# Retention and two mixture-of-experts layers on one core: domain rows, bank sums, low parts, gate passes and tables

## Chip, cores and metric

One core of a Trainium2 chip runs the whole kernel in one launch. The metric is the device time of that launch in microseconds (us). The engines by their names in the profile: PE (TensorE, matmul), DVE (VectorE), ACT (ScalarE), POOL (GpSimd) and SP (SyncE, which here issues every DMA). PEld is PE's weight load, which runs beside the matmuls. A "q" behind an engine's name marks its sequencer (SPq issues DMAs).

## What is computed

```python
def _attn_ref(q, k, v):                 # q, k, v: (2, 8, 768, 64)
    ...
    for t in range(S):
        state = gamma[None, :, None, None] * state + np.einsum('bhd,bhe->bhde', k[:, :, t], v[:, :, t])
        y[:, :, t] = scale * np.einsum('bhd,bhde->bhe', q[:, :, t], state)

def _moe_ref(x, w_gate, w1, w2):        # x: (1536, 512), 8 experts of 512 x 1024 and 1024 x 512
    logits = x @ w_gate
    logits = logits - logits.max()
    P = np.exp(logits)
    for _ in range(8):
        P /= P.sum(1, keepdims=True) + 1e-09
        P /= P.sum(0, keepdims=True) + 1e-09
        P *= N / E
    for e in range(E):
        out += P[:, e:e + 1] * (np.maximum(x @ w1[e], 0.0) @ w2[e])

def _moe2_ref(x, domain_probs, w1, w2): # 4 experts of the same size
    p = domain_probs / (domain_probs.sum(-1, keepdims=True) + 1e-09)
    for e in range(E):
        out += p[:, e:e + 1] * (np.maximum(x @ w1[e], 0.0) @ w2[e])
```

Retention gives x, the first layer takes it, the second takes the first one's output.

## The kernel before

**Retention.** Twelve chunks of 128 positions, six for each of the two sequences (NCK = 6). Round i of the loop (L369 to L398) scales the running state (`att_decay`, POOL), loads and prepares chunk i+2 (`load_att`, `att_prep`: ACT copies q into a padded tile qab, POOL makes ks and qs), computes the scores of chunk i+1 (`att_scores`: PE L251, DVE mask L252), adds chunk i to the state (`att_state`: PE L271, DVE L279 or L284) and computes its outputs (`att_out`: PE L295 and L298) into one of two PSUM banks called chain. The first chunk of a sequence (0 and 6) has no L295, the last (5 and 11) no state. What turns outputs into the first layer's x runs one or two rounds later: `todo[:4]` reads the bank (`first_half` for the first three chunks of a sequence; b12, a split, `sums13`, `sums24` with L152 for the others), `late` splits the sums TA and TB, which then lie in SBUF, into a high part (ACT, L77) and a low part (L78).

**Number format.** Every operand of the expert matmuls is split into a high part and the rest, so that one product is three matmuls (L494). The products of 2 x 2 blocks are made with seven instead of eight multiplications; the sums for that are `+S..`, `+T..` for the weights (`sum_of`, L117), TA and TB for x. `split_hi` (ACT, L124) and `split_lo` (L128) split the weights. The lows of A11, A22, A12 and S1 of the very first weights run on DVE, S2, S3 and S4 on POOL.

**Order.** The code is written in the order in which each engine runs it: every engine takes its instructions strictly in that order, and SP its DMAs. In the retention the order is the loop's. Behind it each call is an event with a position in slots; one slot is one group of six matmuls (about 1.04 us), a unit has 28 slots. A unit is half an expert's hidden width for one sequence, 48 in all; unit k begins at position 28k. First come seven products M1 to M7, with r = 0 and 1, then N1 to N7; helpers between them on DVE, ACT and POOL have fitted positions (`UNIT_AT`, `W_AT`). Named in what follows: m22 (POOL, L617, multiplies by the factors, whose tile is also the high part of A12), h12 and l12 (high part on ACT, low part on POOL, L554, of A12), a4, l3, l4 (DVE), u2 and c1n (ACT copies), e2 to e7 (`add`, bank into the accumulator), g11 (DVE, writes the temporary a11).

**Around the retention's end.** x of chunks 10 and 11 isn't finished in the loop: eight calls left over run in unit 0 at -1, -0.5, 0, 0.5 and 13.8 to 16.8 (L874). Their TA and TB tiles are the accumulators' buffers, which unit 0's e6, e5, e4 and e2 overwrite.

**Gate.** `gate_steps` is a generator that runs in the slots of units 0 to 3 (`GATE_AT`): logits, exponential by a polynomial, then eight passes of row sum and division (L454 to L457), column sum by a matmul with ones (L462) and division (L464 to L468). A pass takes five of these slots. At its end `keep_rows` transposes the factors and writes them to DRAM with eight DMAs (L317), at position 22.9 of unit 3. Unit 4, the first of expert 1, reads them back as rows broadcast over the partitions (`fac`, L526, at position 24 of unit 3). The w2 weights of unit 4 are loaded at 25.1. All these DMAs are SP's.

**Domain factors.** `load_small` and `prep_small` do the same for the second layer's factors in rounds 1 and 4, with eight row DMAs in round 4.

**Tables.** `small` holds identity (128 columns), ones (128) and the decay tables and selector (20); it comes with one DMA between the first loads.

## Time and profile before

| | |
|---|---|
| median of 3 runs | 1535.44 us (1533.57 to 1536.02) |
| the profiled execution's own time, its span | 1535.97 us, 1534.0 us |
| mean granted clock of PE | 0.992 |
| busy, of the span | PE 98%, PEld 95%, DVE 72%, ACT 49%, POOL 68% |
| chain of work that ended last, by engine | PE 86%, POOL 5%, DVE 4%, issue 2%, DMA 1%, ACT 1%, SPq 1% |
| retention | 0 to 86.7 us |
| units 0 to 3 with the gate | 86.7 to 230 us |

How to read it: a busy PE is one with a matmul under way; the granted clock beside it says at which speed. A stage table gives per stretch of time how long each engine was busy. A timeline row names start, length, engine, line, operation and tiles, and in brackets how long the engine was idle before it and which instruction ended that wait. A wait for several things is put down to the one that came last.

### The profile page before, as it was taken

To read this page: it belongs to the slowest core of one execution; us is meant where nothing else is said; L and a number is where in the kernel's file an instruction comes from. 1 tells how busy PE (TensorE), PEld (TensorE's weight loads), DVE (VectorE), ACT (ScalarE), POOL (GpSimd) and SP (SyncE) were. 2 spreads that over 40 slices of the span, in tenths; PEclk is the share of its full clock that TensorE was granted. 3 is DMA by queue.
4 is the path that set the end of the run, shared out by engine and by line. 5 is a ranking of instruction groups with operands and counts; after the bars stand their busy time and mean duration, and the time that the engine had idled before them with its cause. 6 is when DMAs were issued, how large, how long until landed. Compare 5 with 4: busy or idle time off the path is not lost.

```text
span 1534.0 us, 24223 instructions
## 1 busy us (share of the span) xinstructions
PE 1497.3 (98%) x8682; PEld 1463.1 (95%) x8682; DVE 1106.0 (72%) x2096; ACT 755.7 (49%) x1612; POOL 1037.6 (68%) x903
## 2 busy tenths in 40 slices
PE   9799998999999999999999999998999999999998
PEld 6589898999999999999999999998999999999998
DVE  4765986777677677677677767779767777776776
ACT  3454433554554445455455455456655544554452
POOL 5374756867667668668668568569977676686682
PEclk9899999999999999999999999999999999999999
DMA  7410102212111211211211211211121111112112
GB/s 238 139 34 15 49 9 72 63 39 66 49 38 54 61 38 45 70 38 38 77 38 39 76 39 39 63 52 38 39 72 43 38 57 58 38 47 68 38 39 93
DMA packets 97289, 86.23 MB, mean 56 GB/s; under 512 B 9233, under 2 KB 85137, under 8 KB 97169
## 3 DMA queue, kind: packets, MB, share of 16 engines
q1 hardware_dynamic: 97168, 84.69, 18.2%
q8 instruction: 68, 1.11, 0.3%
q14 instruction: 53, 0.43, 0.1%
HBM read 81.45 MB, written 3.22 MB: 55 GB/s over the span
## 4 chain that ended last, share of the span: by engine, by line
PE 86%; POOL 5%; DVE 4%; issue 2%; DMA 1%; ACT 1%; SPq 1%; DVEq 0%; POOLq 0%; ACTq 0%
PE ps L494 47%; PE chain L494 36%; POOL w L128 1%; POOL raw L117 1%; POOL h L554 1%; DMA q<-in_qT 1%; PE chain L295 1%; PE ps L251 1%; PE chain L298 1%; DVE ps L481 1%; DVE acc L481 1%; PE ps L349 1%; DMA raw<-in_w2a 0%; POOL ev L617 0%; DVE acc L152 0%
## 5 line engine op out<-in xcount | busy, mean ns | idle before, releaser
L494 PE MATMUL ps<-h,w 128*128 128x384 f32 x2304 | 433.7, 335 | 4.7 <-POOL h L554 4.4
L494 PE MATMUL ps<-xh,w 128*128 128x384 f32 x1536 | 429.9, 335 | 1.6 <-ACT ev L478 1.6
L494 PEld LDWEIGHTS ps<-h,w 128*128 128x128 f32 x2304 | 402.1, 188 | 7.9 <-POOL h L554 6.4
L128 POOL TENSOR_TENSOR w<-raw,w 128x512 fp32r<-128x512 f32 x262 | 349.7, 1339 | 61.2 <-ACT w L124 61.1
L494 PE MATMUL chain<-xh,w 128*128 128x384 f32 x1152 | 333.3, 336 | 7.1 <-ACT ev L478 5.5
L494 PE MATMUL chain<-h,w 128*128 128x384 f32 x1728 | 334.5, 336 | 3.9 <-DVE acc L481 2.5
L554 POOL TENSOR_TENSOR h<-ev,h 128x384 fp32r<-128x384 f32 x288 | 292.5, 1030 | 44.3 <-ACT h L478 44.2
L494 PEld LDWEIGHTS chain<-h,w 128*128 128x128 f32 x1728 | 303.0, 189 | 6.2 <-DVE acc L481 3.7
L617 POOL TENSOR_TENSOR ev<-ev,fac 128x384 f32<-128x384 f32 x96 | 98.3, 1024 | 306.3 <-DVE ps L613 305.6
L494 PEld LDWEIGHTS ps<-xh,w 128*128 128x128 f32 x1536 | 282.0, 189 | 2.3 <-ACT ev L478 2.3
L124 ACT ACTIVATE w<-raw 128x512 fp32r<-128x512 f32 x336 | 205.1, 624 | 157.9 <-POOL raw L117 133.1
L117 POOL TENSOR_TENSOR raw<-raw 128x512 f32<-128x512 f32 x188 | 244.5, 1300 | 21.1 <-POOL w L128 13.0
L494 PE MATMUL ps<-xl,w 128*128 128x384 f32 x768 | 257.3, 335 | 0.0
L481 DVE TENSOR_TENSOR acc<-chain,acc 128x384 f32<-128x384 f32 x272 | 150.6, 554 | 106.9 <-PE chain L494 105.6
L494 PEld LDWEIGHTS chain<-xh,w 128*128 128x128 f32 x1152 | 211.9, 188 | 9.8 <-ACT ev L478 6.4
L554 DVE TENSOR_TENSOR h<-ps,h 128x384 fp32r<-128x384 f32 x384 | 211.0, 550 | 13.7 <-ACT h L478 4.6
L478 ACT ACTIVATE h<-ps 128x384 fp32r<-128x384 f32 x384 | 186.1, 487 | 65.3 <-DVE ps L481 61.7
L494 PE MATMUL chain<-xl,w 128*128 128x384 f32 x576 | 193.1, 335 | 1.8 <-POOL xl L758 1.8
L478 ACT ACTIVATE chain<-ps 128x384 f32<-128x384 f32 x192 | 91.9, 479 | 206.6 <-DVE acc L481 182.2
L481 DVE TENSOR_TENSOR acc<-ps,acc 128x384 f32<-128x384 f32 x272 | 145.4, 548 | 46.6 <-PE ps L494 46.6
L478 ACT ACTIVATE h<-ev 128x384 fp32r<-128x384 f32 x288 | 149.7, 520 | 46.4 <-DVE ev L557 40.9
L494 PEld LDWEIGHTS ps<-xl,w 128*128 128x128 f32 x768 | 144.7, 188 | 0.0
(122 smaller groups left out, 1242.0 us busy)
## 6 DMA issues: line engine op xcount, KB each, us to landing
fac<-rows SPq DMA_DIRECT2D x46, 384.0 KB
raw<-in_w1a SPq DMA_DIRECT2D x128, 128.0 KB
raw<-in_w2a SPq DMA_DIRECT2D x64, 256.0 KB
raw<-in_w1b SPq DMA_DIRECT2D x64, 128.0 KB
raw<-in_w2b SPq DMA_DIRECT2D x32, 256.0 KB
q<-in_qT SPq DMA_DIRECT2D x12, 256.0 KB
k<-in_kT SPq DMA_DIRECT2D x12, 256.0 KB
v<-in_vN SPq DMA_DIRECT2D x12, 256.0 KB
```

The costliest lines, as they stand in the source:

```text
L117: eng.tensor_tensor(out=raws[s, k], in0=raws[s, a], in1=raws[s, b], op=op)
L124: nc.scalar.activation(out=t[0], in_=raws[s, k], func=AF.Copy)
L128: eng.tensor_tensor(out=lo, in0=raws[s, k], in1=f32(hi), op=ALU.subtract)
L251: nc.tensor.matmul(p_[:, j * 2 * CK:(j + 1) * 2 * CK], t["k"][:, pr, :], z[:, pr], start=True, stop=True)
L295: nc.tensor.matmul(o, S[c % 2][:, pr, :], t["qs"][:, pr, :], start=True, stop=False, skip_group_check=True)
L298: nc.tensor.matmul(o[64 * z:64 * z + 64], t["v"][:, h * 64:(h + 1) * 64], t["a"][:, h, :], start=(c == 0), stop=True, skip_group_check=True)
L349: nc.tensor.matmul(p_[:, 0:TH], l, r, start=(n == 0), stop=(n == len(mm) - 1))
L478: copy, relu = (lambda o, i, f=f: nc.scalar.activation(out=o, in_=i, func=f) for f in (AF.Copy, AF.Relu))
L481: nc.vector.tensor_tensor(out=out, in0=in0, in1=in1, op=op)
L494: nc.tensor.matmul(p_, l, r, start=(first and n == 0), stop=(n == len(mm) - 1), skip_group_check=True)
L554: eng.tensor_tensor(out=lo, in0=src, in1=f32(hi), op=ALU.subtract)
L617: nc.gpsimd.tensor_tensor(out=a22, in0=a22, in1=self.g_[:, 1], op=ALU.mult)
```

## The change

- `prep_small` in round 4 only transposes the domain factors (`turn_rows`); their eight row DMAs are issued at the end of round 7 (NCK + 1), behind the loads of chunk 9.
- In the retention loop `todo[:4]` runs ahead of `late`.
- The low parts of TA and TB of chunks 10 and 11 run on DVE instead of POOL, at 15.8, 17.0 (chunk 11), 18.5 and 20.3 (chunk 10).
- The low parts of A11, A22, A12 and S1 of the first weights run on POOL instead of DVE.
- The gate tile G gets a ninth column holding EPS and a further row block holding EPS / 128, so that both sums contain EPS; the sixteen additions L455 and L466 go. Per pass there is one slot less: four.
- The small tables come with two DMAs: 20 columns at the old place, identity and ones behind the loads of chunk 1.

```diff
@@ -143,7 +143,7 @@
-    def second_half(key, b, j, pb, xa, xb, b21, eng):
+    def second_half(key, b, j, pb, xa, xb, b21):
@@ -163,7 +163,7 @@
         return [b12, lambda: split(*x["B22"], pb[:, 2:4]), sums13, sums24,
-                lambda: split(*x["TA"], xa, eng), lambda: split(*x["TB"], xb, eng)]
+                lambda: split(*x["TA"], xa), lambda: split(*x["TB"], xb)]
@@ -208,7 +208,7 @@
         small = per.tile([P, C_END - C_ID], F32, name="small")
-        nc.sync.dma_start(out=small, in_=cst[:, C_ID:C_END])
+        nc.sync.dma_start(out=small[:, C_G - C_ID:], in_=cst[:, C_G:C_END])
         ident = small[:, 0:P]
@@ -219,6 +219,7 @@
         load_att(1, ("kn", "v"))
+        nc.sync.dma_start(out=small[:, 0:C_G - C_ID], in_=cst[:, C_ID:C_G])
@@ -302,14 +303,17 @@
             xa = xs.pop(i - TPH)
-            return second_half(1, b, c - TPH, quads(p_), xa, xs.pop(i), xa[:, 2:4], nc.gpsimd if i >= len(chunks) - 2 else nc.vector)
+            return second_half(1, b, c - TPH, quads(p_), xa, xs.pop(i), xa[:, 2:4])
-        def keep_rows(t, key, tmp):
+        def turn_rows(t, tmp):
             nc.vector.transpose(tmp, t.rearrange("p t e -> p e t"))
+            return tmp
+        def keep_rows(key, tmp):
             to = rows[key].rearrange("(c f) (t q i) -> q f t c i", f=2, q=4, i=32)
@@ -335,7 +339,7 @@
             nc.vector.tensor_tensor(out=dp_[:, 0:NT], in0=dpr, in1=s.unsqueeze(2).to_broadcast([P, NT, E2]), op=ALU.mult)
-            keep_rows(dp_, 2, ap1.tile([P, 16 * E2], F32, name="dpt"))
+            return turn_rows(dp_, ap1.tile([P, 16 * E2], F32, name="dpt"))
@@ -375,7 +379,7 @@
             att_state(i)
-            for f in late + todo[:4]:
+            for f in todo[:4] + late:
                 f()
@@ -383,7 +387,9 @@
             if i == 4:
-                prep_small()
+                dpt = prep_small()
+            if i == NCK + 1:
+                keep_rows(2, dpt)
             if i == NCK + 3:
@@ -395,14 +401,17 @@
                     split_hi(0, k)
-                    split_lo(0, k, nc.gpsimd if i > 9 else nc.vector)
+                    split_lo(0, k, nc.gpsimd)
         att.close()
-        G_ = per.tile([P, 16, E1], F32, name="G")
+        G_ = per.tile([P, 16, E1 + 1], F32, name="G")
         nc.gpsimd.memset(G_, 0.0)
-        G = G_[:, 0:NT]
-        Gf = G.rearrange("p t e -> p (t e)")
+        nc.gpsimd.memset(G_[:, 0:NT, E1:], EPS)
+        nc.gpsimd.memset(G_[:, NT:NT + 1, 0:E1], EPS / P)
+        G = G_[:, 0:NT, 0:E1]
@@ -417,10 +426,10 @@
             t = spare(4)
-            r_ = lgs = t[:, 0:NT * E1]
-            n_ = pw = t[:, NT * E1:2 * NT * E1]
-            nc.vector.tensor_copy(lgs, pl)
-            q_ = Gf
+            r_ = lgs = t[:, 0:NT * E1].rearrange("p (t e) -> p t e", e=E1)
+            n_ = pw = t[:, NT * E1:2 * NT * E1].rearrange("p (t e) -> p t e", e=E1)
+            nc.vector.tensor_copy(lgs, pl.rearrange("p (t e) -> p t e", e=E1))
+            q_ = G
             yield
@@ -448,26 +457,23 @@
             stt(out=q_, in0=q_, scalar=1.0, in1=pw, op0=ALU.add, op1=ALU.mult)
-            nc.vector.tensor_tensor(out=Gf, in0=q_, in1=q_, op=ALU.mult)
+            nc.vector.tensor_tensor(out=G, in0=q_, in1=q_, op=ALU.mult)
             yield
             for _ in range(8):
-                nc.vector.tensor_reduce(out=rs, in_=G, axis=AX.X, op=ALU.add)
-                ts(out=rs, in0=rs, scalar1=EPS, scalar2=None, op0=ALU.add)
+                nc.vector.tensor_reduce(out=rs, in_=G_[:, 0:NT], axis=AX.X, op=ALU.add)
                 nc.vector.reciprocal(out=rs, in_=rs)
                 yield
-                yield
-                p_ = pg[:, 0:NT * E1]
-                nc.tensor.matmul(p_, ones, Gf, start=False, stop=True, skip_group_check=True)
+                p_ = pg[:, 0:(NT + 1) * E1]
+                nc.tensor.matmul(p_, ones, G_[:, 0:NT + 1, 0:E1], start=False, stop=True, skip_group_check=True)
                 yield
                 nc.vector.memset(p_, 0.0)
-                ts(out=cs, in0=cs, scalar1=EPS, scalar2=None, op0=ALU.add)
                 nc.vector.reciprocal(out=cs, in_=cs)
                 yield
-            keep_rows(G_, 1, evp.tile([P, 16 * E1], F32, tag="a11", name="gt"))
+            keep_rows(1, turn_rows(G_[:, :, 0:E1], evp.tile([P, 16 * E1], F32, tag="a11", name="gt")))
@@ -871,7 +877,7 @@
                         at(k * L + pos, to_x2, un.b, name, c)
-        for pos, f in zip((-1, -0.5, 0, 0.5, 13.8, 14.8, 15.8, 16.8), todo[:4] + late + todo[4:]):
+        for pos, f in zip((-1, -0.5, 0, 0.5, 15.8, 17.0, 18.5, 20.3), todo + late):
             at(pos, f)
```

## Rows read from the trace of the kernel before

**Rows 1.** Stage table: us; busy PE, PEld, DVE, ACT, POOL (instructions); granted clock; DMA share; GB/s.

```profile
0.00:12.54 12.54, 9.43 (x52) 5.94 (x52) 4.04 (x7) 4.42 (x6) 4.33 (x12) 1.00 0.87 299
12.54:40.25 27.71, 27.70 (x224) 19.36 (x224) 15.77 (x33) 8.94 (x16) 15.88 (x16) 1.00 0.65 195
40.25:46.01 5.76, 0.00 (x0) 0.00 (x0) 0.00 (x0) 1.28 (x3) 0.00 (x0) 0.78 0.56 162
46.01:65.50 19.49, 16.68 (x112) 11.72 (x112) 18.55 (x30) 11.65 (x23) 10.08 (x8) 0.71 0.51 175
111.20:117.74 6.54, 3.86 (x16) 3.84 (x16) 1.83 (x4) 3.05 (x7) 5.98 (x6) 0.80 0.28 81
147.00:229.00 82.00, 76.27 (x430) 72.80 (x429) 70.81 (x162) 38.91 (x85) 51.70 (x45) 1.00 0.09 27
232.80:242.00 9.20, 4.23 (x15) 4.23 (x16) 2.67 (x4) 3.10 (x7) 4.42 (x4) 0.81 0.52 149
319.00:1040.00 721.00, 720.06 (x4150) 719.42 (x4149) 524.34 (x975) 357.22 (x766) 496.22 (x431) 1.00 0.17 51
```

**Rows 2.** Timeline, 30 to 46 us: start, us, engine, line, operation, tiles, [idle before].

```profile
30.09 0.43 SPq L190 DMA_DIRECT2D kn<-in_kN  x1
...
35.69 1.04 POOL L234 TENSOR_TENSOR ks<-kn,small 128x512 f32<-128x512 f32 x1 [4.03 <-DMA kn<-in_kN]
...
38.19 0.30 DVE L312 STREAM_TRANSPOSE dpt<-dp 128x64 f32<-128x64 f32 x1
...
38.52 3.19 SPq L317 DMA_DIRECT2D rows<-dpt  x8
...
41.82 0.36 SPq L190 DMA_DIRECT2D q<-in_qT  x1
...
44.68 0.63 ACT L230 ACTIVATE qab<-q 64x512 f32<-64x512 f32 x1 [10.13 <-DMA q<-in_qT]
...
46.01 3.78 PE L251 MATMUL ps<-qab,k 128*128 128x256 f32 x8 [5.76 <-ACT qab L231]
```

**Rows 3.** Timeline, 46 to 57 us: two pairs of L78, and PE's wait.

```profile
46.64 1.29 DVE L78 TENSOR_TENSOR xl<-acc,xh 128x512 fp32r<-128x512 f32 x2 [6.98 <-ACT xh L77]
...
52.63 2.67 DVE L78 TENSOR_TENSOR xl<-acc,xh 128x512 fp32r<-128x512 f32 x2
...
56.88 0.54 PE L295 MATMUL chain<-qs,S 128*128 128x128 f32 x2 [2.81 <-DVE acc L152]
```

**Rows 4.** Timeline, 105 to 114 us: L78 on POOL, and PE's wait.

```profile
105.66 2.56 POOL L78 TENSOR_TENSOR xl<-acc,xh 128x512 fp32r<-128x512 f32 x2
...
113.90 1.92 PE L494 MATMUL ps<-h,w 128*128 128x384 f32 x8 [2.68 <-POOL h L554]
```

**Rows 5.** Timeline of SP, 225 to 231 us.

```profile
225.72 3.21 SPq L317 DMA_DIRECT2D rows<-gt  x8
229.64 0.88 SPq L526 DMA_DIRECT2D fac<-rows  x2
```

**Rows 6.** Chain that ended last, in order of time: start, us, what.

```profile
5.35 5.75 DMA q<-in_qT
...
230.56 6.13 DMA raw<-in_w2a
```

**Rows 7.** Groups by line and shape, DVE, 0 to 120 us: count | busy, mean ns.

```profile
L252 DVE TENSOR_TENSOR a<-ps,mask 128x512 f32<-128x512 f32 x24 | 15.7, 683 | 14.6 <-PE ps L251 10.8 <-DMA mask<-in_cst 3.8
...
L128 DVE TENSOR_TENSOR w<-raw,w 128x512 fp32r<-128x512 f32 x5 | 4.4, 874 | 0.3 <-ACT w L124 0.3
```

**Rows 8.** Four lines of a gate pass: duration ns min/median/max, first and last start us.

```profile
L455 DVE TENSOR_SCALAR rs<-rs x8: 173/210/960, 136.3 to 218.7; 128x12 f32<-128x12 f32 x8
...
L466 DVE TENSOR_SCALAR cs<-cs x8: 160/329/967, 153.2 to 223.2; 128x8 f32<-128x8 f32 x8
...
L457 DVE TENSOR_TENSOR G<-G,rs x8: 258/258/1034, 136.8 to 219.3; 128x96 f32<-128x96 f32 x8
...
L468 DVE SCALAR_TENSOR_TENSOR G<-G,cs x8: 258/912/1187, 153.6 to 224.2; 128x96 f32<-128x96 f32 x8
```

## The prediction

> **What bounds the kernel now.** I read the stage table first, for TensorE (PE). In the long unit stage it is busy 720.06 of 721.00 us with 4150 matmuls, 0.1735 us each: nothing but its own work bounds it there, and no edit of this change touches that. Time can be won only where PE stands still or runs at the lower of its two clock levels (1.2 instead of 2.4 GHz). The table shows them: 40.25 to 46.01 (PE idle, 5.76 us) with 46.01 to 65.50 behind it (granted clock 0.71); 111.20 to 117.74 (about 16 matmuls in 6.54 us); 147 to 229, the gate passes (PE busy 76.27 of 82.00 us, so 5.7 idle); and 232.80 to 242.00 (15 matmuls in 9.20 us) [rows 1]. For each I then looked up in the timeline which wait ended last.
>
> Places one and two of these are one story. PE waits for ACT's padded q of chunk 7, ACT for the q load. SyncE issued chunk 6's last load at 30.09, and its next instruction is the first domain-row DMA, which needs the transpose made at 38.19; eight issues follow (3.19 us), and only then q of chunk 7 goes out, at 41.82 [rows 2]. The load queued behind the rows is what stops PE. Behind the gap VectorE is busy 18.55 of 19.49 us [rows 1], and at 56.88 PE waits 2.81 us for the L152 sums that free its bank, which stand behind two L78 subtractions of 2.67 us [rows 3].
>
> The third place (unit 0): PE waits 2.68 us at 113.90 for GpSimd's l12, which stands behind four L78 subtractions, 2.56 us for the first two and as much for the others [rows 4]. The last place: the eight gate-row DMAs end at 228.93, the factor loads go at 229.64, the w2 load at 230.56 [rows 5] and its first buffer lands 6.13 us later, at 236.7 [rows 6]; ACT's copy of it stands ahead of u2, for which PE waits.
>
> **Domain rows later, sums first.** The eight row DMAs move from ahead of chunk 7's loads to between chunks 9 and 10. q of chunk 7 can then be issued at about 30.6. It queues behind chunk 6, whose last load lands at 35.69 [rows 2]; at the mean 195 GB/s of that stretch [rows 1] 256 KB more land at about 37. With ACT's two copies (0.63 each [rows 2]) PE has them at 38.4, before it is through with chunk 5 at 40.25: the stop goes, with 1.8 us to spare. At their new place the eight issues (3.19 us) delay q of chunk 10 from about 46 to 49.5, and PE wants that at about 58: no cost; if the cover fails, 3.2 us.
>
> What is late next? From 46.01 to 65.50 PE was busy 16.68 us at a granted clock of 0.71 [rows 1], 11.8 us at full clock. Begun at 40.25 that work would reach the outputs of chunk 8 at 52.1 instead of 65.50.
>
> VectorE goes from 38.42 on without a pause. What it did from 46.01 to 65.50 (18.55 us [rows 1]), less the two low parts that move to GpSimd (0.87 each [rows 7]), less one pair of L78 and the start of a sum that now come behind chunk 8's needs (2.0 and 0.4), plus the masks of chunk 6 (2 x 0.68 [rows 7]), is 15.8 us: 54.2. In it the instructions with SBUF operands alone are short or long: the pair of L78 took 1.29 us at 46.64 and 2.67 at 52.63, when GpSimd was at work [rows 3]. With all of them short (about 3 us less) PE's 52.1 decides; with all long (a second pair and the two L117 sums, 2.8 us more) it is 57.0. So the gain here lies between 8.5 and 13.4 us. I take **11.2**, just under the 11.3 of the measured mixture, since GpSimd, busy 10.08 of 19.49 us there [rows 1], gets A11, A22, A12 and S1 low parts on top (four at 1.28, half of a pair in [rows 4]). Afterwards PE's round of chunk 8 with its logits (some 7 us) lets VectorE catch up, so chunk 9 onwards is as now. The lower clock of 46 to 65 is inside this sum: its cause, the idle 5.76 us, is gone.
>
> Here the Trainium skill speaks against the change. The row shows that VectorE's two-SBUF-operand subtraction doubles beside GpSimd work [rows 3]. SBUF — State Buffer, section "SBUF: two separate sides", calls the pair of ports that both share an exclusive lock that the first to start keeps for the whole instruction. By it every low part sent to GpSimd can hold VectorE for its whole length, which is the first rival below. The trace agrees that such an instruction lengthens; how often it will, it leaves open.
>
> **Tables split.** The small-tables load shrinks at its early place from 138 KB to 6 KB; identity and ones come after chunk 1's loads, one issue more (0.4 us) ahead of chunk 2's v, which PE needs far later. The chain starts with q of chunk 2, issued at 5.35 and landed 5.75 us later [rows 6], in a stretch at 299 GB/s [rows 1]: 132 KB less ahead of it is 0.44 us, and nothing is idle behind it until 40.25. Between 0 (it was waiting for something else) and 0.5: **0.45**.
>
> **x low parts to VectorE (unit 0).** GpSimd loses 4 x 1.28 = 5.1 us right ahead of m22, which h12 and l12 wait for. l12 is then done at about 109.5 instead of 113.8, before PE wants it at 110.3. VectorE gets four L78 of 0.65 to 1.34 (halves of the pairs in [rows 3]), 2.6 to 5.3 us, at positions 15.8 to 20.3; queued behind them are a4, l3 and l4, and ACT's e6, which overwrites what they read. By my order l3 is late by 0.6 to 1.0 us for N7. PE lost 6.54 - 16 x 0.1735 = 3.8 us here, idle and lower clock together [rows 1], and half a microsecond more to 119. Gain 1.0 (VectorE takes GpSimd's place) to 4.3; taken **3.5**, since the rows show the lower clock only behind stops of 2.7 us and more [rows 1, 4].
>
> **Gate passes.** Sixteen additions of EPS go: 8 of L455 and 8 of L466, minimum 0.17 and 0.16 us, median 0.21 and 0.33, maximum 0.96 and 0.97 [rows 8]: 2.7 us at the least, 4.3 at the medians. But a pass now has four slots instead of five, so three passes instead of two fall into the crowded end of unit 1 (positions 15 to 27), as many as now into unit 2, none into unit 3. Of a pass stay the two instructions that also lengthen, L457 (0.26 to 1.03) and L468 (median 0.91, up to 1.19), and four that don't (0.8 together): 2.0 to 3.0 us, where it is 0.5 more now at the medians [rows 8]. So unit 1 has 1 to 2 us more work on VectorE, unit 3 some 4 less. The rows now go out twenty slots earlier; the transposed tile shares its buffer with a11, so unit 3's first g11 waits about 1 us for eight issues (3.21 [rows 5]) and their landing, ahead of work that PE wants ten slots later: nothing. The summing matmul reads 104 columns instead of 96: under 0.1 us in all. Of 5.7 us idle I give back **1.0**; bounds -1.5 (crowding) and +3 (half the idle).
>
> **Rows out of the way of w2.** With rows written long before, SyncE waits at the factors only for N7 (done at about 225.5) and the w2 load follows at once. Factors issued at 229.64 had the first w2 buffer landed at 236.7: 7.06 us [rows 5, 6], then ACT 0.64 and u2 0.5. From N7's end PE has six groups of 1.04 us, 6.2 us, until M7 wants u2: 8.2 - 6.2 = 2.0 us stop instead of 5.04. Together with the clock (9.20 - 15 x 0.1735 = 6.6 lost now [rows 1], 1.6 of it clock) the gain is 3.0 to 5.6; taken **4.0**, bounds 1 and 6.
>
> The Trainium skill gives another price: DMA: Bandwidth & Descriptors, section "Anatomy of one DMA — SWDGE (gpsimd) path", fits 2.0 us plus bytes at 436 GB/s; for the 1.04 MB of factors and first buffer that is 4.4 us (an estimate; the section measures another issuing engine), and no stop would be left: 2 us more gain. The trace does not agree, with its own 7.06 us, and that is what I use.
>
> **Sum.** 11.2 + 0.45 + 3.5 + 1.0 + 4.0 = 20.15 us. The profiled execution is 1535.97 (span 1534.0 and 1.97 around it), 0.53 above the median 1535.44; the changed kernel's profiled run comes to 1515.8, its median to **1515.3**.
>
> **Rivals.** (a) VectorE and GpSimd take the place of SyncE in the retention. GpSimd holds A22 and A12 (2.6 us, more when held) ahead of chunk 8's decay, and VectorE's long forms add up; the outputs of chunk 9 then wait some 2.5 us (two low parts) beyond the long end: 8.5 - 2.5 = 6 in place of 11.2, so 1520.5. For it: VectorE's 18.55 of 19.49 [rows 1]. Against: the round with logits leaves it time to catch up. (The Trainium skill's lock rule, above, speaks for it.) (b) The gate crowds: unit 1 and 2 lose 5 us more instead of 1 less: 1521.3. (c) All covers hold: 13.4 + 0.5 + 4.3 + 3 + 5.6 = 26.8, 1508.6. (d) The early q load doesn't come early, because something else than the rows holds SyncE at 30.5: the four other terms alone, 8.95, so 1526.5. Against: nothing stands between in SyncE's rows [rows 2]. (e) Slower: VectorE cannot finish a pass in its four slots (4.2 us), and PE waits at each summing matmul. A unit's own work takes 0.73 of VectorE's time (524.34 of 721.00 [rows 1]), 3.05 us of the 4.2; with both locked forms at their maximum a pass is 3.0, 1.9 short, and a stop of 2.68 us cost 1.1 more by the clock [rows 1, 4]: 3 us a pass, 24 over all eight, less the other 19: 1540.4. It decides once more than 2.5 us is lost in each of the eight. Against: by the same count today's passes (up to 5 and 3.8 in 5.2) are further short, and PE idles only 5.7 us in 82, since VectorE catches up between the crowded ends.
>
> **How the numbers follow.** Forecast 0.67, (a) 0.11, (b) 0.07, (c) 0.09, (d) 0.03, (e) 0.03. The forecast's own terms move it by some 5 us to either side; with (a), (b) and most of (c) the range is 1508 to 1522.5. 0.2%, 3.1 us, is about what a measurement of this kernel can tell from no change. Faster by more than that: all but (e) and a little for a cause not seen, 0.95; within it 0.02; slower 0.03.
>
> **What would show it.** Right: no idle PE at chunk 7's scores, clock 1.00 through the retention, unit 0 starting about 11.6 us earlier; chunk 7's q issued near 31, the domain rows near 46. In unit 0 no wait for GpSimd over 1 us. L455 and L466 gone, the gate rows some 20 slots before the factors. At unit 4's start a stop of about 2 us. Wrong: a wait for VectorE or GpSimd of over 3 us in chunks 7 to 9; the q load still late; PE waiting for G at the summing matmuls; the stop at the w2 load unchanged, which would mean that another queue than the rows held it.

## The result, and the profile after

| | before | changed |
|---|---|---|
| median (4 runs each, same chip) | 1534.51 us (1532.51 to 1536.02) | 1518.17 us (1517.74 to 1519.26) |
| ratio, 95% interval | | 0.9895 (0.9878 to 0.9913) |
| the profiled execution, its span | 1535.97, 1534.0 | 1519.26, 1517.4 |

The kernel became 16.3 us faster; 20.15 were forecast. The time lies within the range, but the terms of the sum don't each lie where I put them. PE's expert matmuls (L494, now L500) can be counted: 168 to a unit. Their starts divide both executions into the same pieces of work:

| stretch | before us | changed us | gain | forecast |
|---|---|---|---|---|
| retention, to the first expert matmul | 88.69 | 84.79 | 3.90 | 11.65 (11.2 + 0.45) |
| unit 0 | 42.69 | 38.30 | 4.39 | 3.5 |
| units 1 to 3, the gate | 98.07 | 93.29 | 4.78 | 1.0 |
| first half of unit 4, w2 | 21.47 | 17.25 | 4.22 | 4.0 |
| from there to the last matmul | 1278.71 | 1279.08 | -0.37 | 0 |
| sum | | | 16.92 | 20.15 |

The page of the changed kernel: busy times, and the chain of work that ended last by engine.

```profile
PE 1492.5 (98%) x8682; PEld 1459.4 (96%) x8682; DVE 1101.6 (73%) x2080; ACT 756.7 (50%) x1612; POOL 1038.6 (68%) x905
...
PE 89%; POOL 4%; DVE 3%; issue 2%; DMA 1%; SPq 1%; ACT 1%; DVEq 0%; ACTq 0%; POOLq 0%
```

The stage table of the changed kernel (columns as in [rows 1]): first two stretches of the retention, then unit 0, units 1 to 3 and the first half of unit 4.

```profile
46.00:58.00 12.00, 7.21 (x68) 5.01 (x67) 11.84 (x17) 6.09 (x12) 10.40 (x9) 0.94 0.57 183
58.00:66.00 8.00, 8.00 (x33) 5.78 (x33) 6.39 (x9) 1.09 (x2) 2.74 (x3) 0.50 0.13 34
...
84.79:123.09 38.30, 37.22 (x209) 35.08 (x208) 24.89 (x50) 21.07 (x46) 21.12 (x18) 0.96 0.12 34
123.09:216.38 93.29, 90.68 (x520) 89.38 (x521) 76.22 (x184) 48.05 (x103) 59.68 (x52) 1.00 0.11 29
216.38:233.63 17.25, 15.20 (x86) 14.44 (x85) 11.62 (x22) 8.86 (x19) 12.39 (x10) 1.00 0.30 81
```

The same three later stretches of the kernel before.

```profile
88.69:131.38 42.69, 38.93 (x210) 37.05 (x209) 20.34 (x45) 21.00 (x46) 26.09 (x22) 0.92 0.10 29
131.38:229.45 98.07, 92.34 (x521) 88.87 (x521) 84.42 (x200) 47.86 (x103) 59.63 (x52) 1.00 0.08 23
229.45:250.92 21.47, 16.43 (x85) 16.11 (x85) 11.92 (x22) 9.48 (x20) 12.97 (x11) 0.92 0.32 87
```

What the reader is to see: in the retention the 5.76 us of [rows 1] are gone, yet from 46 to 58 PE is busy only 7.21 of 12 us, while VectorE is busy 11.84; and from 58 to 66 PE runs at the lower clock. The timeline of the changed kernel from 27 to 58 us, answering [rows 2] and [rows 3], shows where the new stop comes from.

```profile
30.27 2.87 SPq L190 DMA_DIRECT2D q<-in_qT  x1
...
34.48 0.63 ACT L231 ACTIVATE qab<-q 64x512 f32<-64x512 f32 x1 [8.43 <-DMA q<-in_qT]
...
36.47 0.42 DVE L78 TENSOR_TENSOR xl<-chain,xh 128x256 fp32r<-128x256 f32 x1 [3.65 <-ACT xh L77]
...
45.62 3.85 SPq L321 DMA_DIRECT2D rows<-dpt  x8
...
48.52 2.97 DVE L78 TENSOR_TENSOR xl<-acc,xh 128x512 fp32r<-128x512 f32 x2
...
51.20 1.43 POOL L241 TENSOR_TENSOR qs<-q,qtab 128x512 f32<-128x512 f32 x1 [0.25 <-POOL ks L235]
...
51.41 3.45 DVE L117 TENSOR_TENSOR raw<-raw 128x512 f32<-128x512 f32 x2
...
52.99 3.00 POOL L128 TENSOR_TENSOR w<-raw,w 128x512 fp32r<-128x512 f32 x2 [0.36 <-ACT w L124]
...
54.79 1.27 DVE L253 TENSOR_TENSOR a<-ps,mask 128x512 f32<-128x512 f32 x2
55.99 0.84 DVE L285 TENSOR_TENSOR S<-ps,sg 64x256 f32<-64x256 f32 x2
56.87 0.69 DVE L78 TENSOR_TENSOR xl<-chain,xh 128x512 fp32r<-128x512 f32 x1
...
57.70 0.77 PE L296 MATMUL chain<-qs,S 128*128 128x128 f32 x2 [3.73 <-DVE xl L78]
```

Chunk 7's q goes out at 30.27 and the domain rows at 45.62, both as forecast (31 and 46). PE passes chunk 7's scores without the old stop, and then waits 3.73 us ahead of chunk 8's outputs for the bank that VectorE reads at 56.87. VectorE comes to that late: ahead of it stand a late pair (the L78 low parts of TA and TB, 2.97 us) and the L117 pair that makes S3 and S1 (3.45 us; it was 1.42 before, at 57.83), both beside work on GpSimd. Chunk 8's outputs begin at 57.70, 7.8 us ahead of the 65.50 of before; in the 10 us behind, the granted clock is 0.55, which costs 4.5 us, and of the 7.8 only 3.9 are left at the first unit. (Ahead of chunk 7's outputs PE waits 1.05 us, at 48.24, also for VectorE.)

### The profile page after: what moved, and what is told of

The parts are those of the page before. It is cut to its first block, busy times and chain, and to the rows that moved or that the text cites. A ratio compares the mean times of both kernels' runs of the same rounds, so it can differ in the third digit from the quotient of the medians.

```text
span 1517.4 us, 24216 instructions
## 1 busy us (share of the span) xinstructions
PE 1492.5 (98%) x8682; PEld 1459.4 (96%) x8682; DVE 1101.6 (73%) x2080; ACT 756.7 (50%) x1612; POOL 1038.6 (68%) x905
## 4 chain that ended last, share of the span: by engine, by line
PE 89%; POOL 4%; DVE 3%; issue 2%; DMA 1%; SPq 1%; ACT 1%; DVEq 0%; ACTq 0%; POOLq 0%
PE ps L500 49%; PE chain L500 37%; POOL w L128 1%; POOL raw L117 1%; DMA q<-in_qT 1%; PE chain L296 1%; POOL h L560 1%; PE chain L299 1%; PE ps L252 1%; PE ps L353 1%; DVE acc L487 1%; POOL xl L764 0%; DVE ps L487 0%; DMA raw<-in_w2a 0%; POOL ev L623 0%
## 5 line engine op out<-in xcount | busy, mean ns | idle before, releaser
L500 PE MATMUL ps<-h,w 128*128 128x384 f32 x2304 | 433.0, 335 | 2.8 <-POOL h L560 2.5
L500 PE MATMUL ps<-xh,w 128*128 128x384 f32 x1536 | 429.9, 335 | 0.5 <-ACT ev L484 0.5
L500 PEld LDWEIGHTS ps<-h,w 128*128 128x128 f32 x2304 | 402.6, 188 | 5.7 <-POOL h L560 4.7
L128 POOL TENSOR_TENSOR w<-raw,w 128x512 fp32r<-128x512 f32 x266 | 355.2, 1339 | 61.1 <-ACT w L124 61.0
L500 PE MATMUL chain<-xh,w 128*128 128x384 f32 x1152 | 333.1, 336 | 4.0 <-ACT ev L484 2.2
L500 PE MATMUL chain<-h,w 128*128 128x384 f32 x1728 | 332.6, 335 | 2.3 <-DVE acc L487 1.8
L500 PEld LDWEIGHTS chain<-h,w 128*128 128x128 f32 x1728 | 301.7, 188 | 4.1 <-DVE acc L487 2.2
L500 PEld LDWEIGHTS ps<-xh,w 128*128 128x128 f32 x1536 | 281.2, 188 | 1.2 <-ACT ev L484 1.2
L117 POOL TENSOR_TENSOR raw<-raw 128x512 f32<-128x512 f32 x188 | 244.1, 1298 | 20.5 <-POOL w L128 14.7
L500 PE MATMUL ps<-xl,w 128*128 128x384 f32 x768 | 256.9, 335 | 0.0
L500 PEld LDWEIGHTS chain<-xh,w 128*128 128x128 f32 x1152 | 211.4, 188 | 6.8 <-ACT ev L484 3.0
L500 PE MATMUL chain<-xl,w 128*128 128x384 f32 x576 | 192.9, 335 | 1.4 <-POOL xl L764 1.4
L500 PEld LDWEIGHTS ps<-xl,w 128*128 128x128 f32 x768 | 144.4, 188 | 0.0
```

The costliest lines, as they stand in the source:

```text
L117: eng.tensor_tensor(out=raws[s, k], in0=raws[s, a], in1=raws[s, b], op=op)
L128: eng.tensor_tensor(out=lo, in0=raws[s, k], in1=f32(hi), op=ALU.subtract)
L500: nc.tensor.matmul(p_, l, r, start=(first and n == 0), stop=(n == len(mm) - 1), skip_group_check=True)
```

## Experiments

Ratios are to the kernel before on the same chip (medians there 1536.2, 1536.5 and 1534.39 us, for three groups of four kernels each).

**The rows alone.** The kernel before, with the eight row DMAs moved and nothing else.

```diff
             if i == 4:
-                prep_small()
+                dpt = prep_small()
+            if i == NCK + 1:
+                keep_rows(2, dpt)
```

> The kernel before with one part of the change: the eight domain-row DMAs go out behind chunk 9's loads; nothing else differs. All theories: the 5.76 us stop at chunk 7's scores goes. The late split pairs still run ahead of the bank's reading and the low parts of A11, A22, A12 stay on VectorE. Theory L (GpSimd's low parts lengthen VectorE's sums): the pair of L117 stays near 1.4 us, VectorE frees chunk 8's bank at about 57.6 - 2.0 + 0.7 + 2.4 = 58.7 us, the retention ends at about 84.5 (2.2 us before the kernel before), time 1532. Rival W (VectorE simply has too much ahead of the bank, whoever takes the low parts): the L117 pair is 2.5 us or more, bank at 60.7, retention ends at 86 to 87, time within 1 us of before. My own forecast's step (8.5 us and more from the rows) would need an end at 78 or earlier.

Measured: 1528.28 us, ratio 0.9948 (0.9930 to 0.9966); the first expert matmul at 81.34. That is 7.35 us ahead of the kernel before, more than either theory gave, and less than my own step. Timeline, VectorE and PE:

```profile
45.76 2.14 DVE L78 TENSOR_TENSOR xl<-acc,xh 128x512 fp32r<-128x512 f32 x2
...
49.48 0.46 PE L295 MATMUL chain<-qs,S 128*128 128x128 f32 x2 [2.48 <-DVE acc L152]
...
50.43 1.42 DVE L117 TENSOR_TENSOR raw<-raw 128x512 f32<-128x512 f32 x2
```

The L117 pair stays short with GpSimd quiet, as theory L says; the stop comes at chunk 7's outputs, behind a late pair, and not at chunk 8's. Moving the rows alone brings in the retention, in this one execution, no less than the whole change brought (81.34 against 84.79).

**Low parts back on VectorE.**

```diff
-                    split_lo(0, k, nc.gpsimd)
+                    split_lo(0, k, nc.gpsimd if i > 9 else nc.vector)
```

> The changed kernel with the low parts of A11, A22, A12 and S1 back on VectorE. Theory L: without GpSimd's two low parts beside it the L117 pair falls from 3.45 to about 1.4 us, VectorE gets A11's low part (0.7) ahead of it; the stop at chunk 8's outputs falls from 3.73 to about 2.4 us, the clock still falls behind it; retention ends at 82 to 83 us, time 1517 to 1518.5. Rival W: other GpSimd work (the decay, ks, qs) lengthens the pair as well, it stays over 2.5 us, and the 0.7 to 0.9 us of each low part come on top: stop of 4.4 us or more, retention ends at 84.5 or later, time 1520 or more.

Measured: 1516.22 us, 0.9869 (0.9854 to 0.9885); first expert matmul at 82.38, a stop of 2.93 us at chunk 8. The L117 pair took 2.38 us, between the two theories: without a low part beside it the second sum is short (0.69), the first is still long (1.66) beside GpSimd's qs.

**The order back.**

```diff
-            for f in todo[:4] + late:
+            for f in late + todo[:4]:
```

> The changed kernel with the old order in the retention: the late split pairs run ahead of the bank's reading again. Theory O (sums first was worth what I gave it): each bank is read one pair of L78 later (2.5 to 3.0 us); the stop ahead of chunk 8 grows from 3.73 to about 6 us, chunk 7's from 1.05 to 3.5; retention ends at 87 us or later, time 1522 or more. Rival M (the stop only moves): as in the run with the rows alone, PE stops for chunk 7's bank instead (2.5 to 3.5 us), the clock falls there and is back before chunk 8's logits, and VectorE catches up meanwhile; retention ends at 81.5 to 83.5 us, time 1517 to 1519.

Measured: 1515.26 us, 0.9864 (0.9843 to 0.9885); first expert matmul at 81.91. Rival M is right in its mechanism: the stop only moves, to 49.97 (2.71 us, chunk 7), and the time is 1.7 us under its range; theory O is out.

**The changed kernel again.**

> The changed kernel once more, unchanged. Three kernels with the same instructions in the retention had their first unit at 80.6, 83.4 and 84.0 us, the changed kernel's profile had it at 84.8, and chunk 6's q reached ACT at 32.8 to 34.5. If that is how far one execution is from another, this one's first unit lies between 80 and 85, its time within 1517 to 1520. It sets how much the runs with the low parts back and with the old order (82.4 and 81.9) can say: if it comes at 82.5 or earlier, those two differ from the changed kernel by no more than two executions of it do.

Measured: 1516.21 us, 0.9876 (0.9859 to 0.9894); first expert matmul at 83.36, with a stop of 4.47 us at chunk 8.

```profile
38.16 1.25 DVE L253 TENSOR_TENSOR a<-ps,mask 128x512 f32<-128x512 f32 x2
...
55.31 0.69 DVE L78 TENSOR_TENSOR xl<-chain,xh 128x512 fp32r<-128x512 f32 x1
```

With the two kernels below that differ only behind the retention there are five executions of one retention: 80.60, 83.36, 83.43, 83.96 and 84.79. ACT had chunk 6's q at 32.5 to 34.5 in them. The time, 1516.21, lies a little under the 1517 to 1520 expected. So 82.38 and 81.91 of the last two experiments lie inside what one kernel does from run to run: neither the low parts on GpSimd nor the order, each undone by itself, is shown to change the time.

**The sums a round later.** S3 and S1, and all that follows from them, move one round on; round 9 had none.

```diff
-        FIRST_W1 = {6: ("A11", "+S3", "+S1"), 7: ("A22", "+S2", "A12"), 8: ("+S4", "S1"), 9: (), 10: ...
+        FIRST_W1 = {7: ("A11", "+S3", "+S1"), 8: ("A22", "+S2", "A12"), 9: ("+S4", "S1"), 10: ...
```

> The changed kernel with the first weights' sums and splits (A11, S3, S1; A22, S2, A12; S4, S1) one round later each, so that the L117 pair no longer stands ahead of chunk 8's masks, state sum and bank on VectorE. Theory P (place: the pair of 3.45 us is what chunk 8 waits for, and the halved clock of 7.8 us behind the stop is the stop's price): VectorE frees the bank about 3.4 us earlier, at 54.1; the stop falls from 3.73 to 0.5 us or less, granted clock 1.00 instead of 0.50 behind it; the retention ends at about 82.8 - 3.4 - 3.9 = 75.5 us, time about 1511. Rival W (VectorE has too much work altogether): the stop comes back at chunk 9 or 10 with 3 us and more and the clock with it; retention ends at 80 or later, time 1515 to 1518.

Measured: 1509.54 us, 0.9825 (0.9810 to 0.9841); first expert matmul at 75.68, outside the five executions above by 4.9 us (two more executions of this retention, in the last two runs below, have 75.25 and 79.34). Stage table and timeline of VectorE:

```profile
46.00:58.00 12.00, 11.64 (x100) 8.56 (x99) 11.84 (x20) 6.42 (x13) 8.73 (x8) 1.00 0.63 192
58.00:66.00 8.00, 8.00 (x62) 6.25 (x62) 5.48 (x8) 4.07 (x8) 5.23 (x4) 1.00 0.01 4
```

```profile
47.58 1.28 DVE L78 TENSOR_TENSOR xl<-acc,xh 128x512 fp32r<-128x512 f32 x2
48.78 1.27 DVE L253 TENSOR_TENSOR a<-ps,mask 128x512 f32<-128x512 f32 x2
49.98 0.84 DVE L285 TENSOR_TENSOR S<-ps,sg 64x256 f32<-64x256 f32 x2
50.86 0.69 DVE L78 TENSOR_TENSOR xl<-chain,xh 128x512 fp32r<-128x512 f32 x1
51.47 3.01 DVE L78 TENSOR_TENSOR xl<-acc,xh 128x512 fp32r<-128x512 f32 x2
54.40 1.40 DVE L117 TENSOR_TENSOR raw<-raw 128x512 f32<-128x512 f32 x2
```

VectorE is as busy from 46 to 58 as in the changed kernel (11.84 us), but it reads the bank at 50.86 instead of 56.87, and the pair comes behind it. PE is busy 11.64 instead of 7.21 us and the clock stays at 1.00. Of the 6.0 us by which the bank is read earlier, 3.4 are the pair and 1.7 the L78 pair ahead of the masks, which is short here (1.28 us against 2.97); the rest is an earlier start. Theory P is shown, rival W is out: there was time enough on VectorE, in the wrong order. The edit moves the first weights' splits on ACT and low parts on GpSimd along with the sums; which share those have is not separated, except that taking the low parts alone from GpSimd, above, changed nothing that could be measured.

**The sums a round later, with the old order.** The same edit, and `late + todo[:4]`.

> The sums and splits a round later as before, but the old order: late split pairs ahead of the bank's reading. Theory O: with the L117 pair out of the way sums first is what keeps PE running; with the old order each bank is read 2.1 to 3.0 us later, PE stops 2 to 3 us ahead of chunk 7's or 8's outputs, the clock falls behind it for 3 to 5 us of loss; first unit at 80 to 82 us instead of 75.7, time 1514 to 1516. Rival: moving the L117 pair is enough by itself, the order is worth nothing: first unit at 77 or earlier, time 1509 to 1511.

Measured: 1516.43 us, 0.9874 (0.9855 to 0.9894); first expert matmul at 84.09. Timeline, VectorE and PE:

```profile
47.23 2.43 DVE L78 TENSOR_TENSOR xl<-acc,xh 128x512 fp32r<-128x512 f32 x2
...
51.23 0.46 PE L296 MATMUL chain<-qs,S 128*128 128x128 f32 x2 [2.78 <-DVE acc L152]
```

Theory O's mechanism holds here; the first unit comes 2 us later than it said, 1.40 of which PE had already waited at 36.34 for ACT's copies of chunk 6's q. So sums first and the moved pair work only together: with one of the two, or neither, PE stops 2.7 to 4.5 us for VectorE at chunk 7 or 8 and the clock falls; with both it waits for VectorE there at most 0.36 us, in three executions. In the change as it was made the first of them stood alone.

**The w1 load later.**

```diff
-            if i == 3:
+            if i == 4:
                 load_w1(0)
```

> The changed kernel with the first w1 load (1 MB, eight DMAs) in round 4 instead of round 3, behind chunk 6's loads instead of ahead of them. Theory S (late start): in the changed kernel chunk 6's q, issued at 28.16, reached ACT at 34.48, 1.9 us later than before, because the w1 load and chunk 7's loads run beside it; VectorE's row of work without a pause began at 36.47 instead of 34.58. With the w1 load behind, ACT has q by 32.6 or earlier, VectorE's row begins at 34.6 or earlier, the stop at chunk 8 falls from 3.73 to 1.8 us or less; retention ends at 79 to 81, time 1514.5 to 1516.5. Rival: the start is set by PE or ACT and not by the load, or the w1 pieces now come late for A11's split at 45.9 and L117 waits: stop the same or longer, time 1517.5 to 1521.

Measured: 1519.35 us, 0.9887 (0.9871 to 0.9902). VectorE's row of work began at 33.30, as theory S says, and then broke off:

```profile
42.02 0.42 DVE L78 TENSOR_TENSOR xl<-chain,xh 128x256 fp32r<-128x256 f32 x1 [3.84 <-ACT xh L77]
```

ACT's L77 stood behind chunk 7's q, now the one that comes late (PE waits 1.02 us for it at 41.36), and PE stopped 2.88 us at 50.26. In these two orders the q that comes late is the one issued behind the 1 MB of w1; moving the load won nothing (first expert matmul at 83.43).

**Low parts of x back on GpSimd** (old positions and order of the eight calls left over).

```diff
-        for pos, f in zip((-1, -0.5, 0, 0.5, 15.8, 17.0, 18.5, 20.3), todo + late):
+        for pos, f in zip((-1, -0.5, 0, 0.5, 13.8, 14.8, 15.8, 16.8), todo[:4] + late + todo[4:]):
```

> The changed kernel with the low parts of TA and TB of chunks 10 and 11 back on GpSimd at their old positions and in the old order. Theory G (GpSimd's four instructions ahead of m22 were the cause): PE waits 2.5 us or more for GpSimd's l12 in unit 0 and the clock falls behind it; 4.4 us lost there, time about 1522.6. Rival (the stop in unit 0 was made by something that the earlier retention has moved too): under 1.5 us lost, time 1518 to 1519.7.

Measured: 1522.59 us, 0.9908 (0.9887 to 0.9928). Timeline, GpSimd and PE:

```profile
97.56 2.56 POOL L78 TENSOR_TENSOR xl<-acc,xh 128x512 fp32r<-128x512 f32 x2
...
101.03 2.55 POOL L78 TENSOR_TENSOR xl<-acc,xh 128x512 fp32r<-128x512 f32 x2
...
105.81 1.54 PE L500 MATMUL ps<-h,w 128*128 128x384 f32 x4 [2.66 <-POOL h L560]
```

The wait of [rows 4] is back (2.66 against 2.68 us); unit 0 takes 44.14 us instead of 38.30. Theory G is shown, with 5.8 us against the 4.4 expected; its earliest retention of the five, 80.60, hides 4 us of that in the time of its profiled execution.

**Five slots for a pass, additions still gone.**

```diff
                 yield
                 yield
+                yield
                 p_ = pg[:, 0:(NT + 1) * E1]
```

> The changed kernel with five instead of four slots for a gate pass, the sixteen additions still gone. The gate rows then go out as late as before, just ahead of the factors, and the w2 load behind them: the stop at unit 4's start should return from 1.77 to about 5 us with its clock, 4.2 us. Theory D (the fewer VectorE instructions gave the gate's 4.8 us): nothing else is lost, time about 1518.2 + 4.2 = 1522.4. Theory F (that the passes end before the end of unit 3 gave it): another 2.5 us in the last 15 us of unit 3, time about 1525.

Measured: 1520.20 us, 0.9892 (0.9875 to 0.9909). Timeline, SP and PE:

```profile
209.92 3.20 SPq L321 DMA_DIRECT2D rows<-gt  x8
213.90 0.87 SPq L533 DMA_DIRECT2D fac<-rows  x2
214.83 2.04 SPq L98 DMA_DIRECT2D raw<-in_w2a  x4
...
221.93 0.69 PE L501 MATMUL chain<-xh,w 128*128 128x384 f32 x1 [4.89 <-ACT ev L485]
```

Units 1 to 3 take 91.99 us (121.76 to 213.75): 6.1 less than before, 1.3 less than with four slots. The first half of unit 4 takes 21.62 (17.25 with four). So theory D is right about the gate: the additions give its gain, and the time lies 2.2 us under the 1522.4 that D gave. The four slots cost 1.3 us of it by crowding and win 4.4 behind, where the stop of 4.89 us is back with a clock of 0.50 just behind it (0.84 over the half unit).

**w2 ahead of the factors**, and three runs together. The edit is one line; the next kernel joins it to the sums a round later; the last also gives the first five passes five slots.

```diff
-                    at(k * L + LOAD_AT[2], load_w2, un.s)
+                    at(k * L + (-4.5 if un.u == 1 and un.g == 0 else LOAD_AT[2]), load_w2, un.s)
```

> The changed kernel with the w2 load of unit 4 at position -4.5, ahead of the two factor loads that wait for N7's end. Theory Q (the 1.77 us stop at unit 4's start is the w2 load queued behind the factors): the first w2 buffer lands several us earlier, the stop goes, time about 1518.2 - 1.8 = 1516.4. Rival: the load waits at its later pieces for raw buffers still in use, the factors behind it come late, and g12 or the scaling of the accumulators stops PE instead: time 1518 or more.

Measured: 1517.35 us, 0.9873 (0.9856 to 0.9890). The half unit takes 16.44 us instead of 17.25; the stop of 1.77 became two of 0.52 and 0.66 that wait for VectorE and ACT. Both sides were partly right: 0.8 us, not 1.8. It is read from the half unit alone (17.19 to 17.36 in six kernels and repeats with the old load place and a clock of 1.00); the time doesn't tell it from the changed kernel's 0.9895 and 0.9876.

> The first weights' sums and splits a round later and the w2 load of unit 4 ahead of the factors, together. If both act in their own places they add up: the retention as in the run with the sums alone (no stop over 0.5 us, clock 1.00), 0.8 us less around unit 4's start: about 1509.5 - 0.8 = 1508.7 us. If the earlier retention brings another wait there, 1509.5 or more.

Measured: 1508.41 us, 0.9827 (0.9812 to 0.9842), first expert matmul at 75.25 and the half unit 16.45. In the profile the two stand side by side, as forecast; the ratio (0.9825 with the sums alone) doesn't show that the second adds anything.

> The same with five slots for the first five gate passes and four for the last three. From the run with five slots for all: in the stretch of the first passes it was 2.6 us shorter than with four (61.4 against 64.0), and lost 5.7 us behind it, because the rows went out late and the w2 load with them. With five slots of 40 added the rows still go out well ahead of N7's end. Theory: the crowding goes (the 1.45 us stop in unit 2 among it) and nothing is lost at unit 4: about 1508.7 - 2.6 = 1506 us. Rival: the crowding only moves to the last passes: 1508 to 1509.

Measured: 1506.83 us, 0.9815 (0.9796 to 0.9834), the intervals of the last two overlap. In its profile units 1 to 3 take 92.16 us against 93.28 with four slots, and the half unit 17.18 against 16.45: the rival, for the most part. Both beat the changed kernel on the same chip (1516.21), by 7.8 and 9.4 us. (The 1.45 us stop that its expectation puts in unit 2 lies in unit 1, at 151.39.) Its retention has the same instructions as that of the run before it and ended 4.1 us later, at 79.34: PE waited 0.95 us for a late q at 36.55 and 1.06 us for GpSimd at 48.98, with a clock of 0.79 behind it. So this retention too varies from run to run.

## Why the prediction was right, and where it wasn't

**Right by its sum, not by its largest term.** 3.2 us are missing, and that is -7.75 in the retention, +0.9 in unit 0, +3.8 in the gate, +0.2 at w2 and -0.4 behind. That the time lies within the range is in good part luck: more than half of what the retention fell short was made good by the gate and unit 0, beyond the bounds that I had given them. By the signs named beforehand the retention was wrong: a wait for VectorE of over 3 us in chunks 7 to 9 (3.73 at chunk 8), a clock of 0.50 behind it instead of 1.00, unit 0 3.9 instead of 11.6 us earlier. The other signs came as forecast.

**The retention** was mis-sized: 3.9 for 11.65. Three steps of it failed.
- VectorE's start. I let it go on from 38.42. It came to the same masks at 40.45, since its row began at 36.47 instead of 34.58, behind a q of chunk 6 that ACT had at 34.48 (32.58 before). Over the five executions it had it at 32.5 to 34.5, so this step is worth 0 to 2 us; why it differs from run to run is not settled. It doesn't make the stop: in the changed kernel's second profile the masks came at 38.16, earlier than I had them, and the bank was still free only at 56.00, with the stop at 4.47 us.
- What VectorE does ahead of the bank. My count of 15.8 us ended with the state sum S; measured it is 16.4 to there (17.1 in the second profile), and 0.7 more for the bank's low part, which PE waits for too. So the sum was 0.6 to 1.3 us short and the end point another 0.7: the bank came free at 57.56, 0.6 beyond even my 57.0 for long forms. Of the pieces, the L117 pair, 3.45 us, is the one that need not stand there.
- The price of the stop that is left. I wrote that PE would be at chunk 8 at 52.1 and VectorE at 54.2, so a stop of some 2 us was in my own numbers, and behind it I took the clock as 1.00, "its cause is gone". [rows 1] put a clock of 0.71 over the whole of 46.01 to 65.50, and I charged all of it to the 5.76 us stop. The row of before at 56.88 [rows 3] already showed a second stop, of 2.81 us, and the 8 us behind it have a clock of 0.57. This step is 3.9 of the missing 7.75 us. The first two and the tables' 0.45 are the rest, since PE came to chunk 8 7.8 us earlier and not 11.65.

The mechanism at chunk 7 was right: its q goes out at 30.27 and the 5.76 us stop is gone. What the retention can give when nothing else stops PE, the run with the sums a round later shows: 88.69 to 75.68 is 13.0 us, within my bounds of 8.5 to 13.9 with the tables. But it needs an edit that the forecast didn't have, so it doesn't bear out the 11.65 for the change as made.

**The rivals.** Rival (a) named the engines, VectorE and GpSimd in SP's place, but put the wait at chunk 9. It came at chunk 8, and the retention's gain, 3.9 us, is less even than the 6 that (a) left it. The Trainium skill (SBUF — State Buffer, section "SBUF: two separate sides") gives the pair of ports to whichever starts first, a VectorE instruction with two SBUF inputs or a GpSimd one that reads SBUF, for its whole instruction. The trace agrees: the first L117 sum began at 51.41, in GpSimd's qs of 51.20 to 52.63, and took 1.77 us, that is 0.55 beyond the end of qs, a little under its short length of 0.69; the masks and the state sum, which read PSUM, stay at 1.27 and 0.84. But with GpSimd's low parts taken away the time did not move measurably; what decided was the place of the pair in the order. Rival (d) is out, chunk 7's q goes out at 30.27; so are (b) and (e), since the gate gained; and (c), the retention's covers did not hold.

**Tables split** is not shown to bring anything. SyncE issues chunk 6's q at 28.16 instead of 28.53, which looks like my 0.45; but the run with the rows alone, whose tables are not split, has it at 28.16 too, and the runs with the split tables and the old place of the w1 load have it anywhere from 28.04 to 28.76. (The early load became 10 KB, not the 6 I wrote; that leaves the 0.44 where it was.)

**Unit 0** gave 4.39, a little beyond the upper bound of 4.3: PE waits nowhere in it for GpSimd over 0.25 us, and the clock where the stop was is 1.00 (107.30 to 115.10). The four L78 on VectorE took 0.84 to 1.41 us each, 4.4 in all, within the 2.6 to 5.3 I gave; the 0.6 to 1.0 us by which l3 was to be late for N7 don't show as a wait of PE. The 4.39 is the stop of 2.68 and one of two stretches at the lower clock, 1.7 us each: before they ran from 115.16 to 118.57, behind the stop, and from 125.40 to 128.81; in the changed kernel one is left, at 117.97.

```profile
114.10 2.84 PE L361 MATMUL chain<-small,acc 16*128 16x8 f32 x24
...
117.97:121.38 3.41, 3.41 (x12) 2.54 (x11) 1.33 (x5) 1.36 (x3) 0.00 (x0) 0.50 0.00 0
```

The first row is from the timeline, the second from a stage table. I had overlooked the stretch at 125.40 when I wrote that the rows show the lower clock only behind stops of 2.7 us and more; it comes behind no stop at all (see the last section).

**The gate** gave 4.78, beyond its bound of 3. The groups of VectorE over units 1 to 3, first before, then changed:

```profile
L468 DVE SCALAR_TENSOR_TENSOR G<-G,cs 128x96 f32<-128x96 f32 x8 | 6.4, 801 | 0.3
L466 DVE TENSOR_SCALAR cs<-cs 128x8 f32<-128x8 f32 x8 | 3.7, 457 | 0.0
L457 DVE TENSOR_TENSOR G<-G,rs 128x96 f32<-128x96 f32 x8 | 3.5, 444 | 0.3
L455 DVE TENSOR_SCALAR rs<-rs 128x12 f32<-128x12 f32 x8 | 3.0, 376 | 0.3
```

```profile
L465 DVE TENSOR_TENSOR G<-G,rs 128x96 f32<-128x96 f32 x8 | 3.5, 440 | 0.3
L474 DVE SCALAR_TENSOR_TENSOR G<-G,cs 128x96 f32<-128x96 f32 x8 | 3.4, 430 | 0.3
```

The sixteen additions had cost 6.7 us, not the 4.3 I summed from medians: where a few instructions take three to five times the median, the sum is count times mean. The division L474 also shrank, from 6.4 to 3.4 (5.0 with five slots, so both the additions and the slots bear on it). VectorE has 8.2 us less to do (84.42 to 76.22), PE 3.1 us less to wait (5.73 to 2.61 idle). The other 1.7 us of the gain are fewer busy us of PE (92.34 to 90.68) for the same products; where they come from is not shown. The crowding that I feared is there, 1.3 us, smaller than the gain. g11 of unit 3 waited 0.93 us for the rows' DMAs, hidden, as forecast.

**w2.** The changed kernel's timeline, SP, ACT and PE, answering [rows 5] and [rows 6]:

```profile
190.81 3.20 SPq L321 DMA_DIRECT2D rows<-gt  x8
213.45 0.87 SPq L532 DMA_DIRECT2D fac<-rows  x2
214.38 2.05 SPq L98 DMA_DIRECT2D raw<-in_w2a  x4
...
220.37 0.63 ACT L124 ACTIVATE w<-raw 128x512 fp32r<-128x512 f32 x1 [4.36 <-DMA raw<-in_w2a]
...
221.43 0.44 PE L500 MATMUL chain<-xh,w 128*128 128x384 f32 x1 [1.77 <-ACT ev L484]
```

From the factors' issue to the first w2 buffer it took 6.92 us (7.06 used), the stop is 1.77 us (2.0 forecast), the clock stays at 1.00, the gain is 4.22 (4.0). The Trainium skill's fit (DMA: Bandwidth & Descriptors, "Anatomy of one DMA — SWDGE (gpsimd) path"), 4.4 us by my estimate, would have left no stop. The trace does not agree: 6.92 us, and a stop.

## What to carry to other kernels

When a stop is removed, ask what stops PE next, and charge that stop with its clock as well as with its length: here a stop of 3.7 us cost 4.5 us more behind it. Look, for the engine that is waited for, through its own order for work that nobody needs yet; the first weights' sums placed a round later won some 8 us, about as much as the whole change in that stage or more. Two edits can be worth nothing singly and much together, so an edit undone by itself is no proof that it does nothing; and instructions that are sometimes held are to be summed by their mean.

## What was not expected of the hardware

One and the same retention ended anywhere between 80.6 and 84.8 us in five executions; the changed kernel's eight times, on two chips, lie between 1513.97 and 1519.26, so this stage may be most of what sets one execution apart from another. The landing of chunk 6's q doesn't order them (ACT had it at 33.65 in the one that ended at 80.60, at 32.84 in the one at 83.43); the shortest has the shortest stop at chunk 8 (2.71 against 3.68 to 4.47 us) and the least loss by the clock behind it. What sets the stop's length from run to run is open. The granted clock in the 8 us that follow the stop, in this stage:

| kernel | stop us | clock, next 8 us | lost us |
|---|---|---|---|
| sums a round later | 0.36 | 1.00 | 0 |
| all three together | 1.06 (for GpSimd) | 0.79 | 1.7 |
| rows alone | 2.48 | 0.57 | 3.4 |
| x low parts back | 2.71 | 0.79 | 1.7 |
| order back | 2.71 | 0.60 | 3.2 |
| old order, sums later | 2.78 | 0.61 | 3.1 |
| before, second stop | 2.81 | 0.57 | 3.4 |
| w1 load later | 2.88 | 0.50 | 4.0 |
| low parts back | 2.93 | 0.50 | 4.0 |
| changed | 3.73 | 0.50 | 4.0 |

(Lost is 8 times one minus the clock; where the clock is 0.50 the lower level lasts beyond the 8 us, and over 10 us 4.5 to 4.9 are lost. The stops of 3.68, 4.15 and 4.47 us in the other executions of the changed retention have 0.50 too.) A stop of 1.06 us was followed by the lower level here, and one of 1.45 us in unit 1 of the changed kernel (at 151.39) was not; two stops of 2.71 us cost 1.7 and 3.2. At unit 4's start eight traces have a stop of 1.72 to 1.86 us; two of them (the two with the sums later and the old load of w2) show the lower level behind it, six don't. What else than the stop's length decides is open.

The clock also fell with no stop ahead of it. In unit 0 of the changed kernel PE is never idle for more than 0.12 us between 86.56 and 117.97, where the lower level begins; what PE ran just before were the 24 small matmuls of L361 (the gate's logits, moving tile 16x8), which ended at 116.94. In 11 of the 14 traces a stretch at the lower level begins during these matmuls or within 1.4 us of their end, in three (w1 load later, order back, sums later with the old order) none does, and there unit 0 takes 36.86 to 36.88 us instead of 38.30. So some 1.4 us are left to be won in that unit; what makes the difference is open.
